# Linear attention and SwiGLU, forward and backward on one core: first stage, turn, tails and squares re-ordered

## The chip, the core and the metric

One Trainium2 chip; the kernel runs on 1 core of it. The metric is device microseconds of one execution. Before: 832.5 us, the median of 4 runs (831.35 to 833.17).

## What is computed

One transformer block and its gradients, in bf16, for S=2048 rows of D=640, with H=32 heads of 20 and F=1728:

```python
phi = lambda t: where(t > 0, t + 1, exp(t)) + 1e-6
q, k, v = split_heads(layernorm(x) @ wqkv)            # linear attention
pq, pk  = phi(q), phi(k)
kv, z   = einsum("hsd,hse->hde", pk, v), pk.sum(over s)
o       = einsum("hqd,hde->hqe", pq, kv) / (einsum("hqd,hd->hq", pq, z) + 1e-6)
h       = x + merge_heads(o) @ wo
n       = layernorm(h)
out     = h + (silu(n @ w1) * (n @ w3)) @ w2           # SwiGLU
# returned: out, and the gradients of x, wqkv, wo, w1, w3, w2 for a given grad_out
```

## The kernel before

Rows come in 16 tiles of 128 (t), columns of D in 5 blocks of 128, mostly used as two halves of 320; F in 14 chunks of 128 (fc), the last of 64; for the MLP, S in four groups of 512 rows (c). TensorE (PE) multiplies, with weights loaded per matmul (PEld); ScalarE (ACT) unloads PSUM, and does exp, relu and sigmoid; VectorE (DVE) does statistics, normalisation and elementwise work; GpSimd (POOL) some small work and a DMA queue; SyncE (SP) most DMAs. The order on every engine is written out by hand: each queue runs in program order, and a tile of a pool with few buffers (`bufs`) makes its next writer wait for its last reader.

**First stage** (L415 to L505). 44 warm-up matmuls of 128 columns (`WARM`, L233, L424) run while x and the weights arrive. Per tile t, `Stats.part` (L144) takes mean and variance of a half on DVE, POOL raises the variance to the power -1/2 (L152), `Stats.norm` (L154) applies both on DVE (`norm_act`, L158 to L160, on ACT for tiles 10, 12 and 14). `p1_tr` (L244) transposes tiles 0 to 7 on PE, copied by ACT (L251) to `pqT`; later tiles are transposed by DMA. `p1_mm` (L258; its matmuls are at L255) multiplies both halves for k into one of two `big` buffers, and `phi` (L269) does exp (L272, to `mq`) and relu (L273, to `rq`) on ACT, with its other half on DVE (`rest`), held back by `phi_rest`. Between: `q_tile` (L299, the same for q) at t = 5, 7, 9, 11; `ghh_chunk` (L368: grad_out times w2 transposed, PSUM tile `gp` in the `big` buffers; its matmuls are at L364) at t = 2 to 5; `m_part` (L380: x transposed times pk, `macc`); the trickle of weight loads (L445), and the tables `stat_of`, `norm_of` (L447 to L450), which say what DVE does in which t.

**Then** (L507 to L556) the last q tiles; `z_late` and `z_row` (L306, L316: sums of pk, spread to all rows as `Zb`, copied by ACT at L324), `r_prod` (POOL) and `r_head` (`r_red`, `r_inv`, `r_scale` on DVE, `r_T` a DMA) for the denominators, and `kvT_block` (L400, matmuls L404), which writes the block-diagonal `bd` through `masked` (L205).

**The turn** (`run(...)`, L782 to L790) is a list of steps. `q_late` is a q tile by halves; `f2_kv` a `kvT_block`; `f2_wT` (matmuls L610) multiplies `bd` with wo, and its transposing DMA on SP fills `Wp`; `f2_half` is half a tile of attention out and the second layernorm's statistics; `f2_hn` normalises, `f2_ht` transposes it on PE (`trh`, L663); `mlp_ghh` is one `ghh_chunk`. Stores and loads stand between.

**MLP loop** (L830 to L873). `mlp` (L681) per (c, fc) does gate and up matmuls and ACT's sigmoids and copies (`gate` at L693); `mlp_pair` (L721) queues 7 DVE operations per pair of chunks, two of which end in a store of 256 KB to `gg_d`: the gate's (L736) by SP's queue, the `ghh` buffer's (L739) by POOL's. `o2_steps` (L741) is the down projection of the group before; its output tile `h2` has two buffers.

**The rest.** w2's gradient (L917 to L960) with `gw2_tail` for the last 64 rows: 80 matmuls of 64 columns, and `gw2_tail_out`, 5 transposes (L932). Then the MLP's backward (`ghn`, L991), attention's backward, `square` and `unload` (L1225 on, L1244, L1268) with five groups of `trk` transposes after them (L1280 to L1284), the loops for k's gradient and x's, and last 40 `grad_job`s of 432 columns (L1179: 16 matmuls at L1189, ACT's copy at L1193, ACT's store at L1194).

Of the kernel before, what the change touches and what calls it, by code (L numbers as in the profile page):

```python
# [9 lines left out]
P = 128  # L10
# [45 lines left out]
def kernel(  # L56
# [73 lines left out]
    class Stats:  # L130
# [13 lines left out]
        def part(self, src, t, j):  # L144
            if j == 0:
                self.st[t] = cp.tile([P, 2, 6], F32, name="st6", bufs=4)
            V.bn_stats(out=self.st[t][:, j, :], in_=src[:, t, j * HD:(j + 1) * HD])
            if j == 0:
                return
            V.bn_aggr(out=self.mv[:, t, :], in_=self.st.pop(t)[:])  # L150
            V.tensor_scalar(out=self.ve[:, t:t + 1], in0=self.mv[:, t, 1:2], scalar1=EPS_LN, scalar2=None, op0=ALU.add)
            G.tensor_tensor(out=self.rs[:, t:t + 1], in0=self.ve[:, t:t + 1], in1=mhalf[:, 0:1], op=ALU.pow)  # L152

# [30 lines left out]
    load_wq(2, 3)  # L184
    load_wq(3, 4)
    load_x(2, 3)
# [46 lines left out]
    WARM = 44  # L233
# [18 lines left out]

    def p1_half(acc, t, n0):
        for c in range(DT):
            T.matmul(acc, lhsT=pqT[:, c, t * P:(t + 1) * P], rhs=wqkv[:, c, n0:n0 + HD], start=(c == 0),  # L255
                     stop=(c == DT - 1))

    def p1_mm(t, n0):  # L258
        acc = ps.tile([P, 2, 512], F32, name="big", bufs=2)
        for j in range(2):  # L260
            p1_half(acc[:, j, 0:HD], t, n0 + j * HD)
        return acc
# [6 lines left out]
    def phi(acc, dst, then=None):  # L269

        mq, rq = (p1.tile([P, D], BF16, name=n, bufs=b) for n, b in (("mq", 3), ("rq", 3)))
        A.activation(two(mq[:]), acc[:, :, 0:HD], AF.Exp)  # L272
        A.activation(two(rq[:]), acc[:, :, 0:HD], AF.Relu)  # L273

        def rest():
            V.tensor_scalar(out=mq[:], in0=mq[:], scalar1=1.0, scalar2=1e-6, op0=ALU.min, op1=ALU.add)
            V.tensor_tensor(out=dst, in0=mq[:], in1=rq[:], op=ALU.add)
            if then is not None:
                then()
# [19 lines left out]
    def q_tile(t):  # L299
        q_home(t)  # L300
        phi(p1_mm(t, 0), pqs[t])
# [66 lines left out]
    def ghh_chunk(n, acc):  # L368

        c, fc = divmod(n, FT)  # L370
        mm5_to(acc, w2T, fc, g2T[c])
# [45 lines left out]
    load_g2T(0)  # L417
    load_w2T(2 * P, 4 * P)
    load_x(8, 12)
# [5 lines left out]
    ln1.run(x_sb, 0, 1)  # L425
    ln1.part(x_sb, 1, 0)
    for a, b in ((0, 2 * P), (2 * P, D)):
        ln1.norm(x_sb[:, 0, a:b], x_sb[:, 0, a:b], 0)
    p1_tr(0, ((0, 2), (2, DT)))
    for t in (1, 2):  # L430
        if t == 1:
            ln1.part(x_sb, t, 1)
            p1_norm(t)
            ln1.run(x_sb, t + 1, t + 2)
        else:
            ln1.part(x_sb, t + 1, 0)
            p1_norm(t)
    ln1.part(x_sb, 3, 1)
    w13 = [go for c0, c1 in ((0, 2), (2, 4), (4, 5)) for go in load_w13(c0, c1)]
    w13 += [lambda: dma(out=w1[:, :, F:FP], in_=rows(B_w3)[:, :, F - FL:F])]  # L440

# [3 lines left out]
    trickle = {3: w13[0], 4: w13[1], 11: lambda: load_wq(4, 6), 12: w13[2], 14: w13[3], 15: load_wo}  # L445

    stat_of = {t: (t + 4,) for t in range(7)}  # L447
    stat_of.update({7: (11, 12), 8: (13,), 9: (14,), 10: (15,)})
    norm_of = {t: (t + 3,) for t in range(8)}
    norm_of.update({8: (11, 12), 9: (13,), 10: (14,), 11: (15,)})  # L450
# [9 lines left out]
    outs = {6: ((group_out, 0),), 7: ((xn_out, 0, dma),), 10: ((group_out, 1), (xn_out, 1, dma)), 13: ((group_out, 2),)}  # L460

    QT = (5, 7, 9, 11)
    for t in range(ST):
        k = p1_mm(t, D)
        if t < 3:
            p1_tr(t + 1, ((0, 2), (2, DT)))
        for n in stat_of.get(t, ()):
            ln1.run(x_sb, n, n + 1)
            if on_act(n):
                ln1.bias(n)  # L470
        for n in norm_of.get(t, ()):
            if not on_act(n):
                p1_norm(n)
        phi_rest(t < 4)
        phi(k, pk_all[:, t, :])
        for n in norm_of.get(t, ()):
            if on_act(n):
                p1_norm(n)
        if t in QT:
            q_tile(QT.index(t))  # L480
        if 2 <= t < 6:
            ghh_chunk(t - 2, ps.tile([P, 2, 512], F32, name="gp", tag="big", bufs=2)[:, 0])
            p1_tr(t + 2)
        if t >= 3:
            m_part(0, [t - 3])
# [7 lines left out]
        if t in trickle:  # L493
            trickle[t]()
# [18 lines left out]
    for go in w13[4:]:  # L513
        go()
    z_late((2, 3, 4), big())
    m_part(2, range(8))
    z_row((0, 1), big())
    z_row((2, 3, 4), big())
# [3 lines left out]
    m_part(2, range(8, ST))  # L522
    m_end(2)
    r_head(0)
    load_w2T(4 * P, 8 * P)
# [26 lines left out]
    r_head(5)  # L552
    r_prod(7)
# [167 lines left out]
    def mlp_pair(c, k, sig, s2, gate, up, gh):  # L721
# [14 lines left out]
        op(gate, gate, gh, to=gg_d, r0=F)  # L736
# [4 lines left out]
    def o2_steps(c, q=dma, tag="o2"):  # L741
# [4 lines left out]
        for n, (i, j, fc) in enumerate(jobs):  # L746
            if fc == 0:
                o2["ps"] = ps.tile([P, 512], F32, name="o2", tag=tag, bufs=2)
                if j == 0:
                    o2["sb"] = pf.tile([P, D], BF16, name="h2", bufs=2)  # L750
            T.matmul(o2["ps"][:, 0:HD], lhsT=hhT[c][:, fc, i * P:(i + 1) * P],  # L751
                     rhs=w2[:, fc, j * HD:(j + 1) * HD], start=(fc == 0), stop=(fc == FT - 1))
            if fc == FT - 1:
# [3 lines left out]
                if j == 1:  # L757
                    q(out=out0S[:, t, :], in_=o2["sb"][:])
# [17 lines left out]
    def run(*steps):  # L776
# [5 lines left out]
    run((q_late, 10, f2_mT), (f2_kv, 2), (f2_kv, 3), (f2_kv, 4), (phi_rest,), (q_late, 11), (f2_wT, 0), (f2_wT, 1),  # L782
        (phi_rest,), (q_late, 12), (f2_wT, 2), (f2_wT, 3), (phi_rest,), (q_late, 13, lambda: f2_wT(4)),
        (r_red, 6), (r_inv, 6), (r_scale, 6), (load_x, 2, 4), (r_T, 6), (q_late, 14), (load_x, 4, 8), (load_g2T, 1), (r_store, 4, 6),
        (mlp_ghh, 4), (q_late, 15),
        (sig_table,), (f2_half, 0, 0), (f2_half, 1, 0), (f2_half, 0, 1), (f2_half, 1, 1), (f2_hn, 0), (mlp_ghh, 5),
        (f2_half, 2, 0), (f2_hn, 1), (f2_m_out,), (load_w2T, 8 * P, 10 * P), (f2_half, 2, 1),
        (f2_ht, 0), (mlp_ghh, 6), (f2_half, 3, 0), (f2_hn, 2), (f2_w_out,), (f2_ht, 1), (f2_half, 3, 1), (phi_rest, 2),
        (q_out, 10, 14), (f2_ht, 2), (f2_hn, 3), (mlp_ghh, 7), (load_w2T, 10 * P, F), (f2_half, 4, 0), (f2_ht, 3),
        (f2_half, 4, 1), (r4_out,), (r_red, 7), (r_inv, 7), (r_scale, 7), (r_T, 7), (r_store, 6, 8), (q_out, 8, 10))  # L790
# [39 lines left out]
    for c in range(SC):  # L830
# [8 lines left out]
        for fc in range(FT):  # L839
# [17 lines left out]
            if fc == 3 and 0 < c < SC - 1:  # L857
                load_g2T(c + 1)
# [58 lines left out]
    gt = ps.tile([P, DT, FL], F32, name="gt", tag="gw", bufs=4)  # L917

    def gw2_tail():

        for c in range(DT):
            for t in range(ST):
                T.matmul(gt[:, c, :], lhsT=g2[:, t, c * P:(c + 1) * P], rhs=hb[3][:, t, P:P + FL],  # L923
                         start=(c == 0 and t == 0), stop=(t == ST - 1), skip_group_check=True)
        sb = br.tile([P, DT, FL], BF16, name="gts")
        A.copy(out=sb[:], in_=gt[:])
        return sb

    def gw2_tail_out(sb):
        tr = ps.tile([P, DT, P], BF16, name="gttr", tag="gw", bufs=4)  # L930
        for c in range(DT):
            T.transpose(tr[:FL, c, :], sb[:, c, :], ident[:])  # L932
        ob = br.tile([P, D], BF16, name="gw2o", bufs=2)
        A.copy(out=ob[:FL].rearrange("p (c n) -> p c n", c=DT), in_=tr[:FL])
        A.dma_start(out=out_6[F - FL:F, :], in_=ob[:FL])

    for fc in range(FT - 1):
        b, i = divmod(fc, 4)
        if fc == FT - 2:
            sb = gw2_tail()  # L940
        acc = ps.tile([P, 2, 512], F32, name="gw", bufs=4)
        for j in range(2):
# [3 lines left out]
            if fc == FT - 2 and j == 0:  # L946
# [477 lines left out]
```

## Time and profile before

| what | us |
|---|---|
| runs | 831.35, 832.46, 832.55, 833.17 (median 832.5) |
| the profiled execution's own time | 831.35 |
| its span | 829.6 |
| around the span | 1.75 |

Busy time by stage, in us:

| stretch of the span | stage | PE | DVE | ACT | POOL |
|---|---|---|---|---|---|
| 0 to 57 | first stage | 54.0 | 43.5 | 39.5 | 16.2 |
| 57 to 76 | last q tiles, z, denominators | 18.7 | 15.7 | 8.6 | 11.9 |
| 76 to 103 | the turn | 25.2 | 22.2 | 20.3 | 7.6 |
| 103 to 345 | MLP | 241.7 | 192.8 | 145.4 | 43.6 |
| 345 to 406 | last down projection, w2's gradient | 61.0 | 1.7 | 8.8 | 0.0 |
| 406 to 560 | MLP and attention backward | 154.0 | 102.3 | 31.6 | 20.2 |
| 560 to 593 | squares | 32.7 | 10.8 | 9.6 | 3.3 |
| 593 to 829.6 | gradients of k, x and the weights | 233.1 | 65.0 | 55.9 | 7.9 |

How to read the profile: "L364 PE MATMUL mm<-g2T,w2T 128*128 128x512 bf16 x5" is five matmuls at line 364 that write tile mm from g2T and w2T, with a 128 by 128 weight and 512 columns. In a timeline a row begins with its start and its busy time; what stands in brackets at its end is how long the engine was idle before it, and what ended the idle time. In the waits, a row gives the engine and its waiting line, what released it, the sum of the waits, their number and the longest. PEld is the loading of weights; SPq, ACTq and POOLq are the issuing of DMAs.

### The profile page before, as it was taken

To read this page: it belongs to the slowest core of one execution; us is meant where nothing else is said; L and a number is where in the kernel's file an instruction comes from. 1 tells how busy PE (TensorE), PEld (TensorE's weight loads), DVE (VectorE), ACT (ScalarE), POOL (GpSimd) and SP (SyncE) were. 2 spreads that over 40 slices of the span, in tenths; PEclk is the share of its full clock that TensorE was granted. 3 is DMA by queue.
4 is the path that set the end of the run, shared out by engine and by line. 5 is a ranking of instruction groups with operands and counts; after the bars stand their busy time and mean duration, and the time that the engine had idled before them with its cause. 6 is when DMAs were issued, how large, how long until landed. Compare 5 with 4: busy or idle time off the path is not lost.

```text
span 829.6 us, 14237 instructions
## 1 busy us (share of the span) xinstructions
PE 820.5 (99%) x5568; PEld 524.1 (63%) x5568; DVE 454.0 (55%) x960; ACT 319.5 (39%) x605; POOL 110.7 (13%) x160
## 2 busy tenths in 40 slices
PE   8999999999999999999999999999999999999998
PEld 6676644555555555777777777777777777555554
DVE  7859787899898666400057777772681545200000
ACT  5855787655555666011121221222212333211111
POOL 2335222122121101000001111110220000000000
PEclk9999999999999999999999999999999999999999
DMA  9799998686474455999767898246997688886761
GB/s 258 210 319 186 215 310 247 218 217 171 135 203 145 132 203 163 214 254 269 219 151 187 183 214 207 66 104 112 240 274 128 160 191 179 209 197 137 169 164 37
DMA packets 323315, 157.59 MB, mean 190 GB/s; under 512 B 235312, under 2 KB 318160, under 8 KB 323248
## 3 DMA queue, kind: packets, MB, share of 16 engines
q1 hardware_dynamic: 293696, 127.73, 64.5%
q0 software_dynamic: 5136, 17.73, 6.1%
q10 hardware_dynamic: 24416, 11.23, 6.1%
q8 instruction: 43, 0.70, 0.4%
q14 instruction: 24, 0.20, 0.1%
HBM read 48.15 MB, written 51.46 MB: 120 GB/s over the span
## 4 chain that ended last, share of the span: by engine, by line
PE 88%; ACT 1%; DMA 1%; DVE 0%; issue 0%; ACTq 0%
PE mm L364 20%; PE job L1189 19%; PE ghn L991 14%; PE gxn L1348 8%; PE o L751 7%; PE gw L944 7%; PE gwo L1076 3%; PE dkv L1292 3%; PE gr L1048 3%; PE at L572 2%; PE mm L255 1%; PE dkv L1221 1%; DMA gg_d<-gate 1%; PE gt L923 0%; PE wt L610 0%; PE gkvT L1238 0%
## 5 line engine op out<-in xcount | busy, mean ns | idle before, releaser
L1189 PE MATMUL job<-gb,hnN 128*128 128x432 bf16 x640 | 117.0, 346 | 0.0
L991 PEld LDWEIGHTS <-ggb 128*128 128x128 bf16 x864 | 84.5, 98 | 32.8
L1189 PEld LDWEIGHTS <-hnN 128*128 128x128 bf16 x640 | 62.6, 98 | 54.1
L364 PE MATMUL mm<-pqT,w 128*128 128x512 bf16 x405 | 93.6, 379 | 0.1
L364 PEld LDWEIGHTS <-w 128*128 128x128 bf16 x540 | 52.8, 98 | 63.4 <-issue 0.3
L1193 ACT CAST obs<-job 128x432 bf16<-128x432 f32 (+1 forms) x60 | 29.2, 486 | 123.1 <-PE job L1189 120.7
L751 PE MATMUL o<-w,hhT 128*128 128x320 bf16 x448 | 67.7, 299 | 0.0
L364 PE MATMUL mm<-g2T,w2T 128*128 128x512 bf16 x260 | 64.6, 379 | 0.3 <-ACT gate L693 0.3
L991 PE MATMUL ghn<-w13a,ggb 128*128 128x320 bf16 x448 | 63.5, 299 | 0.0
L991 PE MATMUL ghn<-w13b,ggb 128*128 128x320 bf16 x416 | 61.4, 299 | 0.0
L751 PEld LDWEIGHTS <-hhT 128*128 128x128 bf16 x448 | 43.8, 98 | 23.8 <-issue 0.2
L944 PE MATMUL gw<-g,hb 128*128 128x320 bf16 x416 | 57.0, 299 | 0.0
L374 ACT CAST ghh<-mm 128x512 bf16<-128x512 f32 x52 | 30.5, 587 | 55.0 <-PE mm L364 54.3
L944 PEld LDWEIGHTS <-hb 128*128 128x128 bf16 x416 | 40.6, 98 | 15.7
L1348 PE MATMUL gxn<-wqT,gT 128*128 128x320 bf16 x320 | 48.7, 299 | 0.0
L1056 POOL TENSOR_TENSOR sz<-Zb,g_h 128x640 f32<-128x640 bf16 x16 | 20.2, 1262 | 199.6 <-DVE g_h L1054 107.7
L691 ACT ACTIVATE sig<-mm 128x512 bf16<-128x512 f32 x56 | 33.5, 599 | 28.3 <-PE mm L364 26.2
L364 PEld LDWEIGHTS <-w2T 128*128 128x128 bf16 x280 | 27.2, 98 | 26.9 <-issue 1.9
L1003 ACT ACTIVATE gs<-ghn 128x640 bf16<-128x640 f32 x16 | 11.3, 704 | 78.6 <-PE ghn L991 78.6
L255 PE MATMUL big<-wqkv,pqT 128*128 128x320 bf16 x260 | 39.4, 299 | 1.1 <-ACT pqT L251 0.6
L255 PEld LDWEIGHTS <-pqT 128*128 128x128 bf16 x320 | 30.5, 98 | 14.5 <-ACT pqT L251 2.2
L1348 PEld LDWEIGHTS <-gT 128*128 128x128 bf16 x320 | 31.3, 98 | 12.2
(196 smaller groups left out, 1253.9 us busy)
## 6 DMA issues: line engine op xcount, KB each, us to landing
hh_d<-hhT SPq DMA_DIRECT2D x24, 256.0 KB, 2.7
gg_d<-gate SPq DMA_DIRECT2D x24, 256.0 KB, 3.4
gg_d<-ghh POOLq DMA_DIRECT2D x24, 256.0 KB, 3.4
ggb<-gg_d SPq DMA_DIRECT2D x6, 896.0 KB, 5.7
ggb<-gg_d SPq DMA_DIRECT2D x6, 832.0 KB, 6.3
out_dram<-obs ACTq DMA_DIRECT2D x40, 108.0 KB, 2.8
x_sb<-in_A_x_dram SPq DMA_DIRECT2D x6, 640.0 KB, 6.2
ggb<-gg_d SPq DMA_DIRECT2D x2, 1728.0 KB, 12.3
```

What stands on the lines that cost most here:

```text
L255: T.matmul(acc, lhsT=pqT[:, c, t * P:(t + 1) * P], rhs=wqkv[:, c, n0:n0 + HD], start=(c == 0), stop=(c == DT - 1))
L364: T.matmul(acc[:], lhsT=w[:, c, fc * P:(fc + 1) * P], rhs=rhs[:, c, :], start=(c == 0), stop=(c == DT - 1))
L374: A.copy(out=ghh[n // 2][:, n % 2, :], in_=acc[:])
L691: A.activation(sig[:, i, :], gp[:], AF.Sigmoid)
L751: T.matmul(o2["ps"][:, 0:HD], lhsT=hhT[c][:, fc, i * P:(i + 1) * P], rhs=w2[:, fc, j * HD:(j + 1) * HD], start=(fc == 0), stop=(fc == FT - 1))
L944: T.matmul(acc[:, j, 0:HD], lhsT=hb[b][:, t, i * P:(i + 1) * P], rhs=g2[:, t, j * HD:(j + 1) * HD], start=(t == 0), stop=(t == ST - 1))
L991: T.matmul(acc[:, j, 0:HD], lhsT=ggb[t // 2][:, k, lo:lo + P], rhs=rhs[:, j * HD:(j + 1) * HD], start=(k == 0), stop=(k == NG - 1))
L1048: T.matmul(gr[t][:, j, 0:HD], lhsT=ghT[t][:, c, :], rhs=wT2[:, c, j * HD:(j + 1) * HD], start=(c == 0), stop=(c == DT - 1))
L1076: T.matmul(acc[m][:, j, 0:n], lhsT=r_sb[:, t, m * P:(m + 1) * P], rhs=g_hx[:, t, j * HD:j * HD + n], start=(t == 0), stop=(t == ST - 1))
L1189: T.matmul(acc[:, 0:n], lhsT=lhs[:, t, m * P:(m + 1) * P], rhs=rhs(t), start=(t == 0), stop=(t == ST - 1))
L1193: A.copy(out=ob, in_=acc[:, 0:n])
L1348: T.matmul(acc[:, j, 0:HD], lhsT=g, rhs=wqT[:, k, j * HD:(j + 1) * HD], start=(k == 0), stop=(k == 14))
```

## The change

It has these parts.

1. *First stage.* 34 warm-ups instead of 44. Tile 2 of x is loaded ahead of a weight block, tiles 8 to 11 ahead of a load of w2. Tiles 0 and 1 are only centred before their transposes (`RAW`); 1/sd is applied by ACT as a scale in `phi`, and x_sb is scaled later (`p1_scale`, "C"). Tile 0's centring is split between DVE and ACT. The first halves of tiles 0 and 1 run ahead of their second halves; the transposes of the next tile stand between the two halves of each later tile up to 6; the relu of tiles 0 to 2 is issued after the copy of the next tile's transposes (`LATE`). DVE's work in each t is a table `v_steps` of statistics (S), normalisation (N), `phi`'s rest (R) and scaling (C). `ghh_chunk`s 0 to 3 are at t = 3 to 6; `m_part(0)` follows a table `M0`; the loads of w1 and w3 go column block by column block.
2. *Between.* `m_part(2)` does 10 tiles ahead of `z_row`, whose two parts share a buffer; a load of w2 is earlier.
3. *Turn.* The list is re-ordered; `r_head(5)` and `r_prod(7)` move into it.
4. *Gate stores* go by POOL's queue instead of SP's; the last group's down projection writes into x_sb instead of `h2`; the loads of grad_out's later groups move (`fc` 6, 3, 3).
5. *Tails by column tiles.* The last `ghh` chunk of each group (64 of 128 columns of the PE array) runs as two matmuls of 256 columns on the two column halves of the array; `gw2_tail` likewise: 32 matmuls of 320 columns on two column halves, without transposes.
6. *Squares.* Each of the five squares is followed by its `trk` transposes and copy; loads of xnT, wqT and m are earlier.
7. *The last* `grad_job` is split into 304 and 128 columns.

```diff
+        def part(self, src, t, j, mid=None):
...
             V.bn_aggr(out=self.mv[:, t, :], in_=self.st.pop(t)[:])
+            if mid is not None:
+                mid()
...
+        def center(self, out, src, t):
+            V.tensor_scalar(out=out, in0=src, scalar1=self.mv[:, t, 0:1], scalar2=None, op0=ALU.subtract)
...
     load_wq(2, 3)
+    load_x(2, 3)
     load_wq(3, 4)
-    load_x(2, 3)
...
-    WARM = 44
+    WARM = 34
+    RAW = 2
+    LATE = 3
...
+    def p1_scale(t):
+        xn = x_sb[:, t, :]
+        V.tensor_scalar(out=xn, in0=xn, scalar1=ln1.rs[:, t:t + 1], scalar2=None, op0=ALU.mult)
...
+    def p1_mm(t, n0, between=None, acc=None):
+        todo = (0, 1) if acc is None else (1,)
+        acc = p1_acc() if acc is None else acc
+        for j in todo:
             p1_half(acc[:, j, 0:HD], t, n0 + j * HD)
+            if j == todo[0] and between is not None and len(todo) == 2:
+                between()
...
+    def phi(acc, dst, t, late=False):
+        kw = dict(scale=ln1.rs[:, t:t + 1]) if t < RAW else {}
+        A.activation(two(mq[:]), acc[:, :, 0:HD], AF.Exp, **kw)
+        def relu():
+            A.activation(two(rq[:]), acc[:, :, 0:HD], AF.Relu, **kw)
+        relu_later.append(relu) if late else relu()
...
     def ghh_chunk(n, acc):
...
+        if fc == FT - 1:
+            gh, hw = ghh[n // 2], W // 2
+            G.memset(gh[FL:, 1, :], 0.0)
+            for d in range(DT):
+                for h in range(2):
+                    T.matmul(acc[h * FL:(h + 1) * FL, 0:hw], lhsT=w2T[:, d, fc * P:fc * P + FL],
+                             rhs=g2T[c][:, d, h * hw:(h + 1) * hw], start=(d == 0), stop=(d == DT - 1))
+            for h in range(2):
+                A.copy(out=gh[:FL, 1, h * hw:(h + 1) * hw], in_=acc[h * FL:(h + 1) * FL, 0:hw])
+            return
...
+    def center_first():
+        V.tensor_scalar(out=nmean[:], in0=ln1.mv[:, 0, 0:1], scalar1=-1.0, scalar2=None, op0=ALU.mult)
+        center(0, 0, 2 * P)
+        A.activation(out=x_sb[:, 0, 2 * P:], in_=x_sb[:, 0, 2 * P:], func=AF.Identity, bias=nmean[:, 0:1])
...
+    ln1.part(x_sb, 0, 0)
+    ln1.part(x_sb, 0, 1, center_first)
+    p1_tr(0, ((0, 2), (2, DT)))
     ln1.part(x_sb, 1, 0)
+    ln1.part(x_sb, 1, 1, lambda: center(1))
...
+    v_steps = {1: (R, ("N", 4)), 2: (("S", 5), R, ("N", 5)), 3: (("S", 6), R, ("N", 6), ("C", 0)),
+               4: (("S", 7), R, ("N", 7), ("C", 1)), 5: (("S", 8), R, ("N", 8), R), 6: (("S", 9), R, ("N", 9), ("S", 10)),
+               7: (R, R, ("S", 11), ("S", 12), ("N", 10)), 8: (("N", 11), R, ("S", 13), ("N", 12)), 9: (R, R, ("S", 14), ("N", 13)),
+               10: (R, ("S", 15), ("N", 14)), 11: (R, R, ("N", 15))}
...
+    M0 = {5: (0,), 6: (1, 2), 7: (3,), 8: (4, 5)}
+    M0.update({t: (t - 3,) for t in range(9, ST)})
     for t in range(ST):
+        def between():
+            if t + 1 < XT_DMA:
+                p1_tr(t + 1)
+            while relu_later:
+                relu_later.pop(0)()
+        if t == 0:
+            first = [p1_acc()]
+            p1_half(first[0][:, 0, 0:HD], 0, D)
+            p1_tr(1)
+            first.append(p1_acc())
+            p1_half(first[1][:, 0, 0:HD], 1, D)
+        elif t == 1:
+            between()
+        k = p1_mm(t, D, between, first[t] if t < 2 else None)
+        phi(k, pk_all[:, t, :], t, t < LATE)
         if t in QT:
             q_tile(QT.index(t))
+        for step in v_steps.get(t, (R,) * (t > 11)):
+            if step is R:
+                phi_rest(len(held) - 1)
+            else:
+                V_OPS[step[0]](step[1])
+        if 3 <= t < 7:
+            ghh_chunk(t - 3, ps.tile([P, 2, 512], F32, name="gp", tag="big", bufs=2)[:, 0])
+        m_part(0, M0.get(t, ()))
...
+    load_w2T(4 * P, 8 * P)
     z_late((2, 3, 4), big())
-    m_part(2, range(8))
-    z_row((0, 1), big())
-    z_row((2, 3, 4), big())
+    m_part(2, range(10))
+    zr = ps.tile([P, 2, 512], F32, name="bigx", tag="big", bufs=2)
+    z_row((0, 1), zr[:, 0])
+    z_row((2, 3, 4), zr[:, 1])
...
-        op(gate, gate, gh, to=gg_d, r0=F)
+        op(gate, gate, gh, to=gg_d, r0=F, q=dmaG)
...
+                    o2["sb"] = x_sb[:, t, :] if c == SC - 1 else pf.tile([P, D], BF16, name="h2", bufs=2)[:]
...
+    run((q_late, 10, f2_mT), (q_late, 11, kv3), (phi_rest,), (r_store, 4, 5),
+        (q_late, 12, lambda: (f2_wT(0), f2_wT(1))), (q_late, 13, lambda: (f2_wT(2), f2_wT(3))), (phi_rest,),
+        (q_late, 14, lambda: f2_wT(4)), (load_x, 2, 4), (r_head, 5), (r_prod, 7), (r_red, 6), (r_inv, 6), (f2_m_out,), (f2_w_out,),
+        (load_x, 4, 8), (q_out, 10, 14), (r_store, 5, 6), (load_w2T, 8 * P, 10 * P), (mlp_ghh, 4), (q_late, 15),
+        (sig_table,), (f2_half, 0, 0), (f2_half, 1, 0), (mlp_ghh, 5), (f2_half, 0, 1), (f2_half, 1, 1), (f2_hn, 0),
+        (f2_half, 2, 0), (f2_hn, 1), (load_w2T, 10 * P, F), (f2_half, 2, 1),
+        (f2_ht, 0), (f2_half, 3, 0), (f2_hn, 2), (f2_half, 3, 1), (mlp_ghh, 6), (f2_ht, 1), (mlp_ghh, 7), (f2_ht, 2),
+        (f2_hn, 3), (f2_half, 4, 0), (f2_ht, 3), (f2_half, 4, 1), (r_scale, 6), (r_T, 6), (r_red, 7), (r_inv, 7),
+        (r_scale, 7), (r_T, 7), (r4_out,), (r_store, 6, 8), (q_out, 8, 10))
...
     def gw2_tail():
...
+        gt = ps.tile([P, 2, 512], F32, name="gt", tag="gw", bufs=4)
+        for t in range(ST):
+            for j in range(2):
+                T.matmul(gt[j * FL:(j + 1) * FL, 0, 0:HD], lhsT=hb[3][:, t, P:P + FL],
+                         rhs=g2[:, t, j * HD:(j + 1) * HD], start=(t == 0), stop=(t == ST - 1))
...
+    load_xnT(3)
+    load_wqT(0)
     fill(4)
...
+    for i, (c, ms) in enumerate(SQ_BLOCKS):
         unload(square(wqT[:, 2 * DT:, :], gkvT, i), gm[:, i, :])
+        tr = ps.tile([P, len(ms), P], BF16, name="trk", tag="dkv", bufs=3)
+        for k, m in enumerate(ms):
+            T.transpose(tr[:, k, :], gkvT[:, m, c * P:(c + 1) * P], ident[:])
+        V.tensor_copy(out=gkv_b[:, c, ms[0] * P:(ms[-1] + 1) * P].rearrange("p (i q) -> p i q", q=P), in_=tr[:])
...
+            last = (i, m) == (len(blocks) - 1, DT - 1)
+            for a, b in ((0, NB - P), (NB - P, NB)) if last else ((0, NB),):
+                grad_job(hnN, m, lambda t: gb[i][:, t, a:b], b - a, out[:, m, f0 + a:f0 + b], A.dma_start)
```

## The prediction

> **What bounds the kernel.** I read the page's first two parts, then the waits of TensorE (PE), then the timeline wherever PE waited.
>
> ```profile
> span 829.6 us, 14237 instructions
> ...
> PE 820.5 (99%) x5568; PEld 524.1 (63%) x5568; DVE 454.0 (55%) x960; ACT 319.5 (39%) x605; POOL 110.7 (13%) x160
> ...
> DVE 7859787899898666400057777772681545200000
> ```
>
> PE is the bound, everywhere but in the first 122 us and in one spot at 589 us: the DVE row shows where another engine is nearly full. The waits of PE (us in total, times, longest):
>
> ```profile
> PE gp L364 <- DMA g2T<-in_grad_out_dram: 0.9, 1, 0.9
> PE wt L610 <- DVE bd L205: 0.7, 1, 0.7
> PE big L255 <- ACT pqT L251: 0.6, 2, 0.3
> PE kv L404 <- DMA mT<-mbs: 0.6, 1, 0.6
> PE trh L663 <- DVE hn L155: 0.4, 1, 0.4
> PE big L255 <- ACT Zb L324: 0.3, 1, 0.3
> PE mm L364 <- ACT gate L693: 0.3, 1, 0.3
> PE trk L1283 <- DVE small L1284: 0.2, 1, 0.2
> ```
>
> These are short because a matmul's row lasts until its result is out. In a stream, matmuls start closer together: 0.136 us for 320 columns, 0.216 for 512, 0.182 for 432, 0.056 for 128. So I measured each stall from start to start, less this spacing. Summed: 3.7 us before 10 us (2.2 of it the 44 warm-up matmuls, which start 0.107 apart), 1.9 from 10 to 20, 0.9 from 20 to 60, 3.5 from 60 to 122, 0.2 at 344, 0.2 at 405, 0.7 at 589, nothing else. The last matmul starts at 825.8; 3.8 us of drain follow. At most some 11 us can be won without taking work from PE.
>
> The sum is made against the profiled execution: 831.35 us, which is its span of 829.6 and 1.75 around it. It is the fastest of the four; the median is 832.5, 1.15 above.
>
> **First stage (0 to 57 us).** The rows that price it:
>
> ```profile
> 9.28 0.72 ACT L272 ACTIVATE mq<-big 128x640 bf16<-128x640 f32 x1
> ...
> 14.41 1.24 PE L364 MATMUL gp<-g2T,w2T 128*128 128x512 bf16 x5 [0.95 <-DMA g2T<-in_grad_out_dram]
> ...
> 57.68 1.52 PE L255 MATMUL big<-wqkv,pqT 128*128 128x320 bf16 x10 [0.29 <-ACT Zb L324]
> ```
>
> On ScalarE (ACT) an exp, a relu or a whole-tile copy of pqT lets the next start 0.60 later (the relu after this exp starts at 9.88) and ends 0.71 after its own start. Ten fewer warm-ups end that row at 4.75. Centring needs no 1/sd, so the first transposes start near 4.8 instead of 5.79. The first half of tile 0 then waits for its weights (landed 5.79) and for ScalarE's centring of 384 columns (about 0.7, from the 0.92 of L160's 640) plus two copies: 5.8 to 6.8. Tile 1's transposes and one whole copy put its first half at 8.05, tile 0's second half at 8.73 to 9.41. ScalarE: exp 0 at 9.60, copy of tile 2 at 10.20, relu 0 from 10.80 to 11.51. "big" has two buffers, so tile 2 waits for relu 0: it starts at 11.56, where before it started at 11.34. From here a ring sets the pace: first half 0.68, five transposes until the last is out 0.47, copy 0.60, the late relu 0.72, 0.05 to PE: 2.52 per tile, for 1.64 of PE work. Tile 3 at 14.08, the first gp at 16.60 (g2T, 14.3, no longer matters), done at 17.66. Before, the same work was done at 17.12: +0.5. For tiles 4 and 5 the transposes and macc no longer stand behind gp: relu ends 1.5 after big, gp covers 1.08; another 0.6 is lost by tile 7. There DVE waits for relu 7 before the statistics of tiles 11 and 12, and ScalarE's norm of tile 12 stands before exp 9: tile 10 is late by some 0.6 more. Against it 0.46, the wait at 57.7: both z_rows share a buffer now, and q_tile(5) takes one long free. Net +1.2. Ends: -4.3 (every stall from 5.8 to 57 gone: 1.5, 1.9, 0.9) and +2.5 (0.2 more for each of the four operations scaled by a pointer, as L160 has over L251's 0.71, 0.6 in all, and the full 0.7 at tile 12). The walk lies nearest to the rows, so I take it.
>
> **The turn (76 to 103 us).**
>
> ```profile
> 78.53 1.11 PE L404 MATMUL kv<-mT,wqkv 128*128 128x160 bf16 x15 [0.57 <-DMA mT<-mbs]
> ...
> 81.72 0.97 PE L610 MATMUL wt<-bd,wo 128*128 128x140 bf16 x12 [0.72 <-DVE bd L205]
> ```
>
> Stalls from start to start: 0.73 before kv, 0.88 and 0.12 at wt, 0.13 at Wp, 0.53 and 0.20 at trh, 0.27 at the first MLP matmul, 0.08 elsewhere: 2.9. After it, kv has another q half (0.68) ahead, and mT's transposing DMA no longer stands behind the w2T load (3.23 of the SP queue at 66.4). Between kv and wt lie two q halves (1.36), and r_head(5), which held DVE for 2.4 there, comes later. The four trh have ghh chunks (1.08) between them. Late next: the first trh follows (2,1), and hn 0 comes out about 0.5 too late by the DVE rows; the 0.27 at the MLP's start has the same cover as before. Left: 0.8; so -2.1 (ends -2.9 and 0, the stalls only moving on). The Wp DMAs still take 1.25 of SP each; the last lands about 1 us before f2_half(0, 1).
>
> **Gate stores from SP to POOL.** The 0.42 stall at 117.2 is the gate buffer's store: its operation ended at 110.94, SP issued at 112.87, it landed at 117.16. POOL is idle there. But ScalarE rewrites the buffer 4.6 to 6.7 us after the operation in pairs 0 to 2, 4 and 5, and ghh stores on POOL landed 2.7 to 6.2 after theirs: two pairs may be late by 0.3 together. POOL issues 28 stores more (0.73 each), with ln_rs and the ghh stores behind them. Net -0.1 (ends -0.4, +1.0).
>
> **Column-tiled tails.** Each of four ghh tails turns 5 matmuls of 512 (1.08) into 5 pairs of 256; gw2's tail turns 80 short matmuls, 5 transposes and two switches (2.33 + 0.47) into 16 pairs of 320. Pairs are not in this trace. The nearest rows are the 64-column transposes:
>
> ```profile
> 405.46 0.30 PEld L932 LDWEIGHTS <-gts 128*64 128x64 bf16 x5 [0.27 <-issue]
> 405.46 0.47 PE L932 MATMUL gttr<-ident,gts 128*64 128x128 bf16 x5
> ```
>
> The gw matmul before them starts at 405.24, the one after at 405.86: going in and coming out cost 0.09 and 0.10. Inside, loads and matmuls follow at 0.056, so a load hides under a matmul of the same column tile. If a pair runs side by side (0.109, 0.136): ghh 0.55 + 0.19, gw2 2.18 + 0.19: -1.4 and -0.4. If one after the other: +0.8 and +1.7. I take pairs at 1.7 times one: ghh 0.64 + 0.19, gw2 2.56 + 0.19: -1.0 and -0.1, so -1.1 (ends -1.8, +2.5). ScalarE's second copy and POOL's memset lie beside other work.
>
> The Trainium skill, "TensorE: Matmul & The Clock Gate", Part 3, speaks against the change: weight loads overlap running matmuls only where row groups differ, and column tiles share theirs. The rows above show loads overlapping; by the rule, with two loads of about 0.11 exposed per pair, the term would be an estimated +1.6 (ghh) and +3.1 (gw2).
>
> **The rest.** The last chunk's h tile is x_sb itself, so the 0.18 at 344 goes. Squares with transposes between them: the 0.7 at 589 (PE waiting for DVE's copies) gets the next square and 1.09 of job as cover: -0.7; the x-transpose and weight loads moved earlier enter a quieter queue. The last job split 304 + 128 adds 0.04 on PE, starts the last matmul 0.17 later, but its result is out 0.13 sooner and the copy takes about 0.27 instead of 0.52 (by 0.43 for 320): -0.2.
>
> ```profile
> 826.16 0.52 ACT L1193 CAST obs<-job 128x432 bf16<-128x432 f32 x1 [2.40 <-PE job L1189]
> 826.71 0.34 ACTq L1194 DMA_DIRECT2D out_dram<-obs  x1
> ```
>
> Together -1.1 (ends -1.2, 0). **Sum:** +1.2 - 2.1 - 0.1 - 1.1 - 1.1 = -3.2: 831.35 becomes 828.15, and against the median 829.3.
>
> **Rivals.**
> - *The first stage does pay* (0.18). If tiles 2 to 4 do not run in the 2.52 ring, about 1.7 is won instead of 1.2 lost: 826.4. For it: 3.1 us of stall lie between 6 and 14.4. Against it: three waits on a relu per tile, priced above.
> - *The pairs run one after the other* (0.11): -1.1 becomes +2.5: 832.9.
> - *The clock stays low longer* (0.10). Matmuls start 0.107 apart until 6.0 and 0.056 apart from 8.3. With warm-up done at 4.75 and gaps until 6.4, the half pace may last to about 9.9: 13 matmuls and 10 transposes (2.3) take twice as long: 831.6. The same page, Part 1, puts the step at about 3.4 us of sustained activity.
> - *The gate stores land late* (0.09), the one that makes it slower. Place: the gate buffer, pairs 0 to 6. The slowest ghh store on POOL landed 7.3 after its operation (337.66 to 344.97). If every gate store did, pairs 0, 1, 2, 4 and 5 would hold ScalarE 1.0, 2.7, 0.6, 1.0 and 1.6: 6.9, and 836.3. It decides from about 6.5 on; against it, the first seven ghh stores took 2.7 to 6.2.
>
> **Numbers.** The forecast, 829.3, has 0.52. The range, 825.4 to 832.9, reaches from the paying first stage with full pairs and an early gate store (826.4 - 0.7 - 0.3) to the serial pairs; the late gate stores and what lies below 825.4 are left out. 0.2% (1.7 us, about what a measurement here can tell from no change) puts the bounds at 830.8 and 834.2. Faster: 0.47 of the forecast, the first rival, and 0.01 of the clock's (if its price is small): 0.66. Slower: the gate stores, 0.09. Same: the rest of the forecast (0.05), the serial pairs, the rest of the clock's: 0.25.
>
> **What would show it.** Starts of big at 11.6 and 14.1 and gp at 16.6, idle before them put down to rq; norm of tile 12 on ScalarE after 35.5; no kv or wt wait, one trh wait; no gate wait at 117; two column-tile matmuls starting within 0.03 of each other, or 0.11 apart; no trk wait. I am wrong if gp starts before 15.5, or if PE waits in the MLP for gate.

## The result, and the profile after

The changed kernel took 836.57 us in the median (37 runs, 831.44 to 843.9), the kernel before 832.19 (58 runs, 830.59 to 838.8). The ratio, taken over all runs of both and not of the two medians, is 1.0046, with a 95% interval of 1.0034 to 1.0057: 0.46% **slower**, where 0.4% faster was forecast, and outside the range. The profiled execution took 836.09.

The head of the page after, and the waits of PE (in total, times, longest):

```profile
span 834.4 us, 14210 instructions
...
PE 817.6 (98%) x5541; PEld 522.7 (63%) x5541; DVE 453.6 (54%) x962; ACT 319.7 (38%) x607; POOL 134.4 (16%) x196
```

```profile
PE big L266 <- ACT rq L295: 3.1, 4, 1.3
PE mm L385 <- ACT gate L749: 2.4, 3, 1.3
PE mm L385 <- ACT up L755: 2.2, 1, 2.2
...
PE gp L385 <- ACT rq L295: 0.7, 1, 0.7
PE trk L1326 <- DVE small L1278: 0.6, 1, 0.6
PE bigx L343 <- ACT Zb L345: 0.5, 1, 0.5
PE trh L719 <- DVE hn L160: 0.4, 1, 0.4
```

PE has 2.9 us less to do and ends 4.7 later. The waits for kv, wt and g2T are gone, as forecast; three kinds are new or larger: for rq, for up and for gate. That PE waits for gate in the MLP was one of the prediction's signs that it is wrong.

The stretches between first matmuls, in us, show where the time went. The turn begins with `q_late(10)`, the MLP with its first gate matmul, the next ones with the first matmuls into `gw`, `ghn` and `gkvT`, and the last stretch with the gradient of x (`gxn`):

| kernel | start of turn | turn | MLP | w2's gradient | to squares | squares | rest | span |
|---|---|---|---|---|---|---|---|---|
| before | 76.07 | 26.81 | 245.55 | 59.62 | 166.82 | 60.40 | 194.34 | 829.6 |
| after | 78.72 | 25.31 | 249.26 | 59.19 | 166.83 | 60.49 | 194.56 | 834.4 |
| difference | +2.65 | -1.50 | +3.71 | -0.43 | 0 | +0.09 | +0.22 | +4.75 |

**First stage, +2.65.** PE and ScalarE in the ring:

```profile
9.74 0.84 PE L266 MATMUL big<-wqkv,pqT 128*128 128x320 bf16 x5
11.85 0.84 PE L266 MATMUL big<-wqkv,pqT 128*128 128x320 bf16 x5 [1.26 <-ACT rq L295]
...
14.45 0.84 PE L266 MATMUL big<-wqkv,pqT 128*128 128x320 bf16 x5 [0.80 <-ACT rq L295]
...
16.95 1.24 PE L385 MATMUL gp<-g2T,w2T 128*128 128x512 bf16 x5 [0.71 <-ACT rq L295]
```

```profile
10.42 0.68 ACT L258 COPY pqT<-tr 128x640 bf16<-128x640 bf16 x1
10.99 0.81 ACT L295 ACTIVATE rq<-big,ln_rs 128x640 bf16<-128x640 f32 x1
11.68 0.80 ACT L292 ACTIVATE mq<-big,ln_rs 128x640 bf16<-128x640 f32 x1
```

The relu stands behind the copy, and tile 2 starts when it is done. The starts 11.85, 14.45 and 16.95 answer to the walk's 11.56, 14.08 and 16.60: 2.5 to 2.6 per tile. Against the kernel before, tile 7 starts 1.41 later (29.32), tile 10 2.49 later (38.84), and the turn 2.65 later.

**MLP, +3.71.** From start to start PE lost 2.41 us at the wait for up and 0.39, 1.02, 0.22 and 1.50 for gate, where before lost 0.42; against it the tails gained 4 x 0.31, and 0.18 went at the last group. The 0.39 follows the up wait directly, with no store in it. At the other three ScalarE's copy to gate waited for the store of that buffer's last content, from pairs 0, 2 and 4:

```profile
121.79 0.59 ACT L749 CAST gate<-mm 128x512 bf16<-128x512 f32 x1 [2.29 <-DMA gg_d<-gate]
...
137.13 0.59 ACT L749 CAST gate<-mm 128x512 bf16<-128x512 f32 x1 [3.11 <-DMA gg_d<-gate]
...
151.27 0.59 ACT L749 CAST gate<-mm 128x512 bf16<-128x512 f32 x1 [2.77 <-DMA gg_d<-gate]
```

The way of the first loss, by the timelines of SP's and POOL's queues, of VectorE, ScalarE and PE:

```profile
91.60 0.89 POOL L673 DMA_DIRECT2D wT_d<-pkx  x1
92.48 0.79 POOL L690 DMA_DIRECT2D pq_d<-pkx  x1
```

```profile
94.94 1.69 SPq L185 DMA_DIRECT2D x_sb<-in_A_x_dram  x1
```

```profile
107.59 0.49 DVE L633 TENSOR_TENSOR x_sb<-at,x_sb 128x320 bf16<-128x320 f32 x1 [4.85 <-DMA x_sb<-in_A_x_dram]
...
110.61 0.87 DVE L364 TENSOR_REDUCE rden<-pr 128x16 f32<-128x320 f32 x2
```

```profile
111.20 0.59 ACT L755 CAST up<-mm 128x512 bf16<-128x512 f32 x1 [4.33 <-POOL ln_rs L154]
```

Stores of 800 and 640 KB go first; the load of x tiles 4 to 7 (640 KB), issued at 94.94, lands at 107.50, 12.6 later. In the kernel before it was issued ahead of those stores and landed after 5.5:

```profile
92.22 0.59 SPq L180 DMA_DIRECT2D x_sb<-in_A_x_dram  x1
```

```profile
97.93 0.91 POOL L617 DMA_DIRECT2D wT_d<-pkx  x1
...
101.51 0.79 POOL L634 DMA_DIRECT2D pq_d<-pkx  x1 [0.40 <-DVE pkx L603]
```

In after, VectorE waits 4.85 for it, and `r_red(7)` is queued behind. The up buffer lies in the released pool where `pr` of `r_prod(7)` lay, so ScalarE's copy of up waits for that reduction (the page names POOL's `ln_rs`, which ended at 111.10; the first half of the reduction ended at 111.09, so the profile alone can't tell them apart, and e14 decides for the buffer), and PE for ScalarE.

**The tails** ran side by side. The columns are start, busy time, and the shape of the weights (128 by 64):

```profile
142.18 0.74 PE L397 MATMUL mm<-g2T,w2T 128*64 128x256 bf16 x10
```

```profile
405.82 2.36 PE L983 MATMUL gt<-g,hb 128*64 128x320 bf16 x32
```

The next matmul starts at 408.12: 16 pairs in 2.3, or 0.144 for a pair of 320 columns, where one alone takes 0.136.

### The profile page after: what moved, and what is told of

Same layout as the page of the kernel before. It is cut to its first block, busy times and chain, and to the rows that moved or that the text cites. A ratio compares the mean times of both kernels' runs of the same rounds, so it can differ in the third digit from the quotient of the medians.

```text
span 834.4 us, 14210 instructions
## 1 busy us (share of the span) xinstructions
PE 817.6 (98%) x5541; PEld 522.7 (63%) x5541; DVE 453.6 (54%) x962; ACT 319.7 (38%) x607; POOL 134.4 (16%) x196
## 4 chain that ended last, share of the span: by engine, by line
PE 89%; DMA 4%; DVE 3%; ACT 2%; issue 1%; POOL 0%; SPq 0%; ACTq 0%; DVEq 0%; POOLq 0%
PE job L1240 19%; PE mm L385 15%; PE ghn L1042 14%; PE gxn L1398 8%; PE o L808 7%; PE gw L997 7%; PE big L266 3%; PE gwo L1127 3%; PE gr L1099 3%; PE dkv L1344 3%; PE macc L416 2%; DMA gg_d<-gate 2%; DMA x_sb<-in_A_x_dram 2%; PE at L628 1%; DVE st L147 1%
## 5 line engine op out<-in xcount | busy, mean ns | idle before, releaser
L1240 PE MATMUL job<-gb,hnN 128*128 128x432 bf16 (+2 forms) x656 | 117.0, 342 | 0.0
L1244 ACT CAST obs<-job 128x432 bf16<-128x432 f32 (+3 forms) x61 | 29.3, 481 | 123.0 <-PE job L1240 123.0
L385 PE MATMUL mm<-g2T,w2T 128*128 128x512 bf16 x240 | 59.6, 379 | 2.2 <-ACT gate L749 2.2
L405 ACT CAST ghh<-mm 128x512 bf16<-128x512 f32 x48 | 28.4, 591 | 46.7 <-PE mm L385 41.4
L385 PEld LDWEIGHTS <-w2T 128*128 128x128 bf16 x260 | 25.4, 98 | 27.0 <-issue 3.9
```

The costliest lines, as they stand in the source:

```text
L385: T.matmul(acc[:], lhsT=w[:, c, fc * P:(fc + 1) * P], rhs=rhs[:, c, :], start=(c == 0), stop=(c == DT - 1))
L405: A.copy(out=ghh[n // 2][:, n % 2, :], in_=acc[:])
L1240: T.matmul(acc[:, 0:n], lhsT=lhs[:, t, m * P:(m + 1) * P], rhs=rhs(t), start=(t == 0), stop=(t == ST - 1))
L1244: A.copy(out=ob, in_=acc[:, 0:n])
```

## The experiments

The ratios are to the kernel before, with 95% intervals; "after" is the changed kernel (1.0046). Lines marked + and - are against the kernel named.

**e1: gate stores on SP** (after).

```diff
-        op(gate, gate, gh, to=gg_d, r0=F, q=dmaG)
+        op(gate, gate, gh, to=gg_d, r0=F)
```

> The changed kernel with the gate stores back on SP's queue. Theory A (the loss has three places: the first stage's ring +2.65, the up copy that waits for r_red(7) behind the late x load +2.8, the gate stores on POOL +2.3 net): ScalarE's waits for gate stores fall from 8.5 us in four places to one of at most 2, PE's gate stalls from 2.7 to about 0.4; the up wait of 2.4 stays; 1.5 to 2.5 us less than the changed kernel's 836.1 of the profiled run, about 834. Rival B (arrivals swing from run to run whatever the queue, and the loss is the first stage): no more than 0.5 less, and gate waits of the same size remain.

836.12, ratio 1.0033 (1.0016 to 1.0050). Against theory A the time hardly moved. Its profiled execution has no gate wait, but the up stall (2.18), behind it eight matmuls of 512 columns at 0.427 instead of 0.216 (the granted clock was 0.90 and 0.76 in the five us on either side of 115), and waits of 0.33 and 1.35 for the `ghT` DMA, ahead of matmuls at 511 and 530, which no other run shows in that place. Since the slow matmuls gave the stores 1.7 more to land, this run does not tell what the queue is worth behind a late x.

**e2: x load ahead of the stores** (after).

```diff
-(load_x, 2, 4), (r_head, 5), ... (f2_w_out,), (load_x, 4, 8), (q_out, 10, 14)
+(load_x, 2, 4), (load_x, 4, 8), (r_head, 5), ... (f2_w_out,), (q_out, 10, 14)
```

> The changed kernel with the load of x tiles 4 to 7 issued right after that of tiles 2 and 3, ahead of r_head(5) and of POOL's stores of m, wT and pq. Theory A: it lands near 97 instead of 107.5, VectorE's wait of 4.85 and PE's stall of 2.4 at the up copy go; about 2.8 less, 833.3. Rival B (the 1.6 MB of stores issued by POOL at 91 to 93 hold every transfer of that stretch back, whichever was issued first): it lands after 103, and at least 1 us of the stall stays.

834.92, 1.0028 (1.0006 to 1.0049). Each theory holds in part: no up stall (MLP 244.30), but the load still took 10.8 (93.81 to 104.64), the one before it 6.3, and PE waited 1.07 and 1.58 in the turn (26.83). The load moved ahead in the list, but not ahead of the stores: SP still had transposing DMAs to issue, so that POOL issued its three stores at 92.18, 92.76 and 93.63, and the load followed 0.2 later. e7 moves the stores instead.

**e3: old first stage** (after, with L141 to L510 of the change undone except the ghh tail).

> The changed kernel with the first stage and what follows to 76 us as before (the turn, tails, gate stores, squares and last job stay changed). Theory A: the turn's first q half starts at 76.1 instead of 78.7, and the time falls by as much, 2.65: 833.5. Rival C (the turn's end waits for loads and stores whose landing does not come earlier when the first stage ends earlier): the stall at the up copy grows by 1 to 2 us, and the time falls by less than 1.5.

829.27, 0.9952 (0.9937 to 0.9967): 7.3 below after, more than either theory. The turn starts at 75.88 and takes 25.13. PE has no up stall, although x still took 9.3 (92.43 to 101.75): VectorE waited 2.12 for it and ScalarE's up copy 1.60 (4.85 and 4.33 in after), and PE, which can fill other mm buffers meanwhile, lost nothing.

**e4: tails alone** (before, with the two tails).

> The kernel before with the column-tiled tails alone. Theory A: pairs run side by side, 0.31 less for each of four ghh tails and 0.44 for gw2's: 1.7 less than before, 0.998 of its time. Rival D (what the tails free on PE is lost to the waits beside them, as ScalarE has one copy more per tail): 0.5 less or nothing.

830.65, 0.9976 (0.9955 to 0.9998). 0.43 less at w2's gradient and 0.31 at each ghh tail: theory A. The profile's MLP takes 245.55, as before, all the same: 0.97 more is a wait for gate at 118 (its store, on SP, landed 6.1 after its issue) and 0.25 more one at the last group. The first lies 19 us ahead of the first tail, so rival D, which put such a loss beside the tails, is not what it shows.

**e5: first stage alone** (before, with what e3 undid).

> The kernel before with the new first stage (and what follows it to 76 us) alone. Theory A2 (the ring costs 2.65 by itself; what the changed kernel lost beyond that came where the new turn met the later first stage, at loads held back by POOL's stores): the first q half of the turn starts 2.6 later than in the kernel before, the time rises by 2 to 3.5, the MLP shows no stall at the up copy. Rival E (the new first stage delays its loads and so brings the MLP's stalls with it, whatever the turn): 5 or more above the kernel before, with stalls of over 1 us in the MLP's first pairs.

835.95, 1.0068 (1.0040 to 1.0096). The turn starts 3.34 later (79.41), and takes 0.55 more. The MLP has no up stall and 245.49: the MLP's losses do not come from the first stage alone, so rival E falls by its place. By its time it nearly came (4.3 against the median of the runs of the kernel before made beside it, 5.7 by the ratio), and A2's bound is exceeded: 0.97 more is a wait for `ghT` at 475, and the rest of the difference stays open.

**e6: relu at once** (after).

```diff
-    LATE = 3
+    LATE = 0
```

> The changed kernel with LATE = 0: each relu right after its exp, ahead of the copy of the next transposes. Theory A2 (the ring first half, transposes, copy, late relu sets 2.52 per tile): the waits of big on rq at tiles 2, 3 and of gp shrink from 1.43, 0.96 and 0.87 to about 0.5 each or less, the first gp starts 1 to 1.5 earlier than 16.95, the first stage ends 1 to 1.5 earlier. Rival F (ScalarE is full there, so that the copy is late in place of the relu): the waits move to pqT, and gp starts within 0.3 of 16.95.

835.44, 1.0043 (1.0023 to 1.0064). Not conclusive by itself: PE's matmuls of 320 columns started 0.267 apart until 13 us, so gp came at 17.83. e10 repeats it. But the run shows something else: with the stores in the order of after and the new first stage, x took 9.3 (95.98 to 105.28), landed 1.15 ahead of the first gate matmul, and PE lost nothing for up.

**e7: stores late** (after).

```diff
-(r_inv, 6), (f2_m_out,), (f2_w_out,), (load_x, 4, 8), (q_out, 10, 14), (r_store, 5, 6)
+(r_inv, 6), (load_x, 4, 8), (r_store, 5, 6)
...
+(f2_m_out,) behind (f2_hn, 1), (f2_w_out,) behind (f2_hn, 2), (q_out, 10, 14) behind (f2_half, 3, 1)
```

> The changed kernel with POOL's stores of m, wT and pq 10 to 13 moved back behind the x load, among the first f2 halves, about where they stood in the kernel before; the x load itself stays in its place. Theory A2 (x of tiles 4 to 7 is late since 1.6 MB of stores go ahead of it): it lands 3 to 6 us after its issue in place of 12.6, no wait at the up copy, and 2 to 4 less than the changed kernel's 836.6 median. Rival G (the load is late because the later first stage pushes all of SP's queue): it still takes over 9, and the stall stays above 1.

831.42, 0.9995 (0.9985 to 1.0005), and 11 runs lie within 2.5 us (830.52 to 832.99), where after has 12.5. x was issued ahead of the stores again and landed at 101.14, in 6.1; the MLP takes 243.73, without an up or gate wait:

```profile
95.03 0.58 SPq L185 DMA_DIRECT2D x_sb<-in_A_x_dram  x1
```

```profile
100.80 0.91 POOL L673 DMA_DIRECT2D wT_d<-pkx  x1
```

Theory A2: the order of three stores is worth 5 us here. Rival G falls.

**e8: the mix** (e3, stores late, both x loads at the head of the turn).

> Everything of the change but the first stage, with the x loads at the head of the turn and POOL's stores late, as in e7_stores_late. Theory A2: x is there long before it is needed; one gate wait of at most 0.7 is left in the MLP; the profiled execution takes 827.5 to 828 and all executions stay within 3 us of it. Rival G: as e3_old_first_stage, 829.3 median with 5 us between the lowest and the highest.

828.99, 0.9970 (0.9958 to 0.9983), 828.51 to 830.19: theory A2's spread, but a profiled execution of 829.1 instead of at most 828. x landed at 85.93 and the MLP took 243.84; but the last Wp transpose took 4.4 (87.94 to 92.35) and PE waited 1.46 for it in the turn (26.70).

**e9: the best** (e3, stores late, half a job between the first two squares, last job whole).

```diff
-        if i > 0:
-            fill(1)
+        fill(1)
```

> The change without its first stage and without the split of the last job, with POOL's stores late and half a job between the first square's transposes and the second square. Theory A2 (from the stretches measured so far: 75.9 to the turn, 25.2 the turn, 243.8 the MLP, 59.2, 166.8, then 59.7 instead of 60.5 for the squares to the x gradient, 194.2): a span of 824.8, 826.5 in all, 0.994 of the kernel before; no trk wait. Rival H (the half job only moves that wait, as it is missing later): the trk wait shrinks but 0.5 or more comes back before the x gradient.

827.19, **0.9939** (0.9919 to 0.9959), 826.53 to 828.74; the span was 825.2 for 824.8 expected, the squares 59.70 for 60.49, without a trk wait.

**e10: e7 with the relu at once.**

> e7_stores_late with LATE = 0. Theory A2 (the late relu sets the ring): the waits on rq before gp sum to 1.0 instead of 3.3; unless the clock is low longer, gp starts 1 to 2 earlier than 16.96 and the time is 1 to 2 below e7's 831.4. Rival F (ScalarE's order only moves the wait to the copies): gp within 0.5 of 16.96, same time as e7.

831.50, 0.9996 (0.9976 to 1.0017). Theory A2 in its place, rival F in the time. gp starts at 15.80, 1.16 earlier than in e7, with the waits on rq at 1.4, although tile 2 waits 1.42 for the copy to pqT in place of the relu. The turn starts at 78.45, 1.41 earlier than in e7, 0.59 of it at tile 14's DMA. The profile then loses 1.07 waiting for `ghT` at 453, and the median is e7's.

**e11: norm of tile 12 behind tile 9's relu** (e10).

> e10 with ScalarE's norm of tile 12 issued one tile later, behind tile 9's exp and relu. Theory A2 (that norm waits 0.98 for VectorE's statistics and holds exp 9, and so tile 10): the 0.91 stall at tile 10 falls to 0.3 or less; 0.6 below e10. Rival I (VectorE is late there anyway, so that tile 12's own transposing load is late instead): the stall moves to tiles 12 or 13, and the time is as e10's.

831.32, 0.9989 (0.9975 to 1.0003). Tile 10's 0.91 went to 0.31, and the wait for a transposing DMA at tile 14 grew from 0.47 to 1.09: the turn starts at 78.42, as in e10. Rival I, with the moved stall at tile 14 instead of 12 or 13.

**e12: gate on SP with the stores late** (e7).

> e7_stores_late with the gate stores on SP's queue. Theory A2 (the gate stores on POOL cost nothing by themselves; the changed kernel's gate waits came from VectorE running two pairs late after the late x load): within 1 us of e7's 831.4, gate waits of PE 0.5 or less. Theory A (the gate stores on POOL cost 2.3): 1.5 or more below e7.

832.69, 1.0002 (0.9986 to 1.0017), 1.3 above e7, where theory A2 allowed 1; the profile's turn starts 1.9 later than e7's, for the half pace shown below. The MLP takes 243.73, as e7's, although the gate stores of pairs 2 and 4 landed 4.2 and 5.0 after their issue here and 7.2 and 6.6 in e7, where ScalarE waited for them: PE's buffers covered that. Where the turn ends undisturbed, the queue of the gate stores is worth nothing either way. Its first stage shows the half pace again, one line of PE's timeline:

```profile
9.43 2.85 PE L266 MATMUL big<-wqkv,pqT 128*128 128x320 bf16 x10 [0.78 <-ACT pqT L258]
```

Ten matmuls that take 1.5 in the same place of after.

**e13: 44 warm-ups** (e11).

> e11 with 44 warm-up matmuls instead of 34. Theory K (ten warm-ups fewer let the half pace of TensorE last longer in some executions: 320-column matmuls started 0.27 apart until 11 to 14 us in three of the nine profiled executions with 34, never past 8 with 44): the upper group of e11's times (831.9 to 833.0, six of twelve) thins out to two or fewer of twelve, the median falls by 0.5 or more although the first transposes come about 0.6 later. Rival L (the gaps after the warm-up decide it, not its length): as many slow starts as with 34, and a median 0.3 to 1 above e11's 831.3.

831.74, 0.9998 (0.9986 to 1.0011); four of twelve above 831.9, and no half pace in the profile. Between the theories, and too few to tell.

**e14: r_red(7) ahead of tile 4** (after).

> The changed kernel with r_red(7) and r_inv(7) ahead of the halves of tile 4, so that VectorE's read of pr is not behind the add that waits for x; stores and x load as in the change. Theory M (the 2.4 stall is the up copy waiting for r_red(7), as its buffer lies where pr lay): x is still late, VectorE still waits, but PE's stall at the up copy falls to under 0.5 and the time by 2 or so. Rival N (the late add itself holds PE, by the at buffers or the operations of the first pairs behind it on VectorE): the stall moves to the gate or to the next pairs, and less than 1 is won.

837.81, 1.0072 (1.0047 to 1.0097). x landed 12.2 after its issue, 4.1 behind the first gate matmul. The waits of PE:

```profile
PE big L266 <- ACT rq L295: 3.1, 4, 1.3
PE mm L385 <- ACT gate L749: 3.1, 1, 3.1
```

The up wait is gone, so it did come from that reduction; but 3.1 for gate stands in its place, as VectorE now comes to the first gate operation 2.9 after ScalarE, and the store later by as much. The profile's MLP took 246.99, 2.3 less than after's, but the median did not fall. Rival N: the buffer is a step of the way, not the cause.

**e15: z_rows in two buffers** (e11, one execution).

```diff
-    zr = ps.tile([P, 2, 512], F32, name="bigx", tag="big", bufs=2)
-    z_row((0, 1), zr[:, 0])
-    z_row((2, 3, 4), zr[:, 1])
+    z_row((0, 1), big())
+    z_row((2, 3, 4), big())
```

> e11 with the two z_rows in buffers of their own again, ten tiles of m_part(2) ahead of them as in the change. Theory O (in a shared tile the second z_row waits for ScalarE's copy of the first): the 0.62 stall there goes, and q_tile(5) waits for a buffer 0.46 or less as in the kernel before; 0.2 to 0.6 less. Rival P: the same 0.6 stands at q_tile(5) instead.

The stall of 0.62 went, and 0.456 stands at `q_tile(5)`, as before. The shared tile costs 0.17.

## Why the prediction was wrong

**The step that failed** is the turn's, "Left: 0.8; so -2.1". Of its stalls on PE 1.45 was left instead of 0.8, so that the turn gained 1.50, up to the first MLP matmul. What failed is what the step put at nothing: of the steps it moved, it followed SP's queue and not POOL's stores. m, wT and pq (1.6 MB) went ahead of the load of x tiles 4 to 7, and no line asked when x is needed. No rival of mine stood at that place. e7 undoes only that and wins 5.1 (836.57 to 831.42); e14 shows that taking away one of the waits behind the late load only shows the next. Whether the order costs anything depends on when x lands: in after, e1 and e14 it came 3.5, 3.2 and 4.1 behind the first gate matmul, and PE lost 2.2 to 3.3 at its first wait in the MLP; in e3 it came 0.7 behind, in e6 and e2 ahead of it, and PE had no up wait. So the old first stage is not needed for that. Why the load took 9.3 in e3 and e6 and 12.6 in after, with the same order, was not tried, nor which of the three stores matters.

In the profiled executions the forecast's -3.2 became +4.7. Of the 7.9 between them, 5.2 are the MLP's waits for up and gate, 1.45 the first stage, 1.2 the rest and 0.6 the turn; the tails took 0.6 off.

**First stage: +1.2, measured +2.65**, and 3.3 to 3.8 in e5 and e7. The mechanism was right (the ring, and ScalarE's norm of tile 12, issued at 36.69 where "after 35.5" was forecast); the terms were too small. By tile 7 it was +1.4 instead of +1.1 (gp 0.35 later than walked, and ended 1.0 instead of 0.5 behind the kernel before); at tile 10 1.1 more instead of 0.6; and the shared z buffer, forecast to win 0.46, lost 0.17 as its second row waits for ScalarE's copy of the first. A wait of 0.4 to 1.2 at tile 14, for its transposing DMA (in e5 for rq), in every run with this stage but the profile of after, was not foreseen. e10 and e11 show two sides of the ring: the relu at once won 1.2 by gp, though tile 2 waited as long for the copy as it had for the relu, and the 0.6 taken away at tile 10 came back at tile 14. Neither moved the median by more than 0.2.

**Gate stores: -0.1.** In e7 and e12 the MLP takes the same time on either queue. In after 1.02, 0.22 and 1.50 were lost for the stores of pairs 0, 2 and 4. The rival "the gate stores land late" was right in the place, and its 836.3 lies within 0.3 of the measured time by luck: with these stores back on SP (e1) the time was 836.12, and with them on POOL and x in time (e7) 831.42. Its price was off: the stores of pairs 2 and 4 landed 9.3 and 6.3 after their issue, and 4.7 and 5.1 in e1 on SP, but the point from which that decides was not 6.5. 9.3 cost PE 0.22, and 7.2 in e7 nothing, while pair 0's 4.8 cost 1.02. That the waits came from stores issued late behind the up stall, and not from slow ones, fits e7 and e14; it was not separated by a run. My expectation of e12, that VectorE ran two pairs late, was wrong for after: its first gate operation (113.28) followed ScalarE's second gate copy at once. In e14 it was late, by 2.9.

**Tails: -1.1, measured -1.67** (1.24 and 0.43): I had taken a pair at 1.7 times one; it took 1.06. The rival of serial pairs is out. The Trainium skill, "TensorE: Matmul & The Clock Gate", Part 3, has weight loads overlap only across row groups. Here both column tiles use all rows, and 32 loads lie within 2.3 us of matmuls, with a pair at 1.06 times one; the measurement decides against the rule, which would set an estimated +3.1 for gw2. The estimate for ghh did not come out of its own working: 0.22 more in each of 20 pairs, on -1.4, is +3.0 and not +1.6.

**The rest: -1.1, measured about 0.1 more.** The 0.18 of the output tile went. The squares did not gain 0.7: after the first square no job follows, and the second trk group waits 0.79 for the buffer of the first square. "Gets the next square and 1.09 of job as cover" was true of the others only; e9 adds the missing half job and gets 0.79 back. The last job's split can't be told from the 0.5 by which that stretch varies between kernels with the same end (194.04 in e12, 194.56 in after).

**The clock rival.** Of 11 profiled executions with 34 warm-ups, four (e1, e6, e12, e15) ran 320-column matmuls 0.267 apart until 11.5 to 13.5 us; in e1 and e12 gp came 1.25 and 2.65 later than in after. Of the six with 44, none went past 7.4. The same page, Part 1, says that the number of matmuls at half pace varies between runs of one kernel; that agrees. The profile of after had none, so it explains none of its 4.75. In e6 and e12 the full pace was not reached before; in e1 and e15 tile 0's first half ran at 0.135, and the half pace came back after the stall of 0.95 behind it. There at least the warm-up was long enough and the gaps behind it are the likelier cause, but after had the same stall without it, and e13 has one profile: it stays open. Open too is what holds the medians of e7, e10, e11 and e13 near 831.5 when single executions reach 829.5.

## What to carry to other kernels

When a list of steps is re-ordered, follow the bytes as well as the instructions: for every load, ask which stores now go ahead of it on any queue, when it lands, and what is queued behind its first reader. Look at when a load lands against the first matmul behind its reader, and not only at how long it took. A wait taken away on a full engine can come back a few tiles on, so undo the parts one at a time and read the stretches: here what e9 keeps was worth 0.61%, and the first stage and the order of three stores hid it. A buffer reused across a pool's release is a wait that no line of the step shows.

## What the runs showed of the hardware

- The x load of 640 KB took 5.5 us in the kernel before and e9 and 6.1 in e7, with the large stores behind it, and 9.3, 9.3, 12.2, 12.6 and 13.3 in e3, e6, e14, after and e1, with 1.4 MB of stores issued by another queue up to 4.3 us ahead. The Trainium skill, "Trainium Kernel Development and Optimization", Key Constraints, says that the queues of SP, ScalarE and GpSimd share the same 16 DMA engines; these rows agree, and do not show it by themselves.
- Two column tiles of 64 run side by side: 0.144 for a pair of 320 columns, 0.136 for one.
- The half pace at the start (0.267 for 320 columns) stood under a granted clock of 1.00 in the rows of e6 and e12; in e1 and e15 the column read 0.50 in the two microseconds inside it (9 to 11, 10 to 12). So the clock column alone can miss it; the spacing does not.
- In e1 PE ran at half pace for eight matmuls after a stall of 2.2 (clock 0.51 from 114 to 116); after stalls of 2.4 in the profile of after and 3.3 in e14 it did not.
